# Decoding seven rows of a weight matrix straight into their buffer, and normalizing a first group of four tiles

## The chip, the cores and the metric

The kernel runs on 1 core of one Trainium2 chip. The metric is device time in microseconds (us); for the kernel before, the median of three runs is 979.46 us (975.63 to 984.27). Besides, one execution was taken by the hardware profiler.

## The reference, cut to what matters

Three layers follow one another on a batch of 4, 768 tokens, 8 heads of 40 (320 channels), all in float32:

```python
for t in range(S):                       # attention: a state per head, 768 steps
    y[:, :, t] = einsum('bhd,bhde->bhe', rt, state)
    Sa = einsum('bhde,bhe->bhd', state, at)
    state = state*wt[:, :, None, :] - einsum(Sa, bt) + einsum(vt, kt)
...
mixed = real(fft(fft(x, axis=1), axis=2))            # second layer
u = x + mixed
un = (u - mean(u)) / sqrt(var(u) + 1e-06)            # over the 320 channels
x = u + maximum(un @ w_ch1, 0) @ w_ch2               # 320 -> 1280 -> 320
...
u = x + (maximum(x.T @ w_tok1, 0) @ w_tok2).T        # third layer
out = u + maximum(u @ w_ch1, 0) @ w_ch2
```

The weights come as 64-bit floats. The kernel decodes each into two 32-bit parts, a rounded high part and the rest, and multiplies with both.

## The kernel before, in words

**Order.** The program is a list of operations (`Plan.op`: engine, cost, function, keys read and written). `Plan.emit` issues them in the sequence of a list written out by hand, `ORDER`: each entry is an operation's number in base 36, with the PSUM buffers that it takes; an entry `+5,acc,0` issues five filler pairs, matmuls of the identity that compute nothing (`warm`, line 54; each pair is two records in the trace). Every engine has its own queue and works it off in this order. An operation of engine `NONE` issues nothing; it opens or closes buffers, and other operations depend on it.

**Attention** (class `Attn`) runs in 12 chunks of 64 tokens, four chunks deep: `load`, `decay`, `kg`, `inv`, `merge`, `chain`, `outp`. Its buffers lie in pools that are closed at three points, the last of which is the operation 'end' in `Mlp.begin` (line 768 and on); the weights of the second layer, W1 and W2, have their buffers only from there on. While the attention runs, `wdec` decodes the first matrix (1280 columns) into DRAM.

**The second layer, per batch b.** `fft` (line 865) builds sums and differences on DVE, splits them into high and low parts (Xh, Xl) and multiplies with a table of cosines and sines on PE in five blocks (four main blocks, line 900, one tail, lines 915 and 916); ACT and DVE copy the result from PSUM into A (lines 925, 926). `fft2` (line 937) does the second transform in four PE groups ('mix', line 947, eight matmuls each) and adds it to x on DVE (line 950), with a sum per token; ACT squares (line 953) and accumulates the variance. Each of the six tiles of 128 tokens of the batch has its column in `sm` and `ss`. Then eight small steps on 6 columns (lines 960 to 967) give the factor `y` = 1/sqrt(var) with one correction step and the shift `nb`; the only ACT function of it is Sqrt (line 961). `norm` and `turnp` (lines 971, 1013) apply them and transpose a group of four tiles on PE (line 1018). `ch` (line 1026) multiplies the group with W1 (line 1047), takes the maximum with 0, splits, and multiplies with W2 (line 1037), ten blocks of 128 hidden channels each; block m reads row m of W2. There are six groups of four tiles; the FFT of the next batch runs inside the loop.

**The second matrix, W2, ten rows of 128 x 320.** `job` (line 844) decodes one row: a load on the SP queue into `mraw` (line 851), two DVE steps that build the value (853, 854), an ACT copy that rounds it to the high part `mdh` (855), two DVE steps for the low bits (856, 857), two POOL steps for the low part (858, 859), and two DMA writes on SP into DRAM (860, 861). There are three sets of buffers; row n uses set n mod 3. After 'end', POOL queues four DMA loads (line 795) that bring W2 back: five rows each of the high and the low part, each waiting for the ten writes of its rows. The third layer's matrices go through the same `job` afterwards.

Of the kernel before, what the change touches and what calls it, by code (L numbers as in the profile page):

```python
# [10 lines left out]
F32 = mybir.dt.float32  # L11
F32R = mybir.dt.float32r
# [84 lines left out]
class Attn:  # L97
    def __init__(s,tc,ident,A,xd,ctx,pctx,xstack,tstack,T1d,W):
# [74 lines left out]
    def decay(s,i):  # L173
# [362 lines left out]
0 1 5 4 2 fg 7 8 6 e 3 9 1b f g h +12,y,0 bx:0 1d 1f 1e a br 3s 1c 3u 8n 3v 3y 3w 7i 3t 7k 3x 3z j bk:1 by bz:0 bl i o m n k bm:1 bn b c d +3,y,0 s:0  # L536
c0 c1:1 l 1g 1h 1i 1l 8l 12:1 13 c2 p:0 1j 1k 40 1q x:2 q r t 1n y 1p bo:0 bp 1m 41 u:1 v w 1o z:0 10 14 15 11 7l +1,y,0 24:1 25 21:1 22 fa:1 fb bq 7m
16 1a 19 18 7n c3:0 c4 7q +1,y,0 1z:0 20 23 1u:2 1v 7r 7s 1w:0 1x 1y 1r:1 1s 26 27 28 1t 17 7o 8o 8p 8q 8v 8u 8t 29 2d 2e 2f 2g 2h 2i 2j 2k 2l 7j 2a
dq 2b 2c 8r fc:1 fd hi c8:1 ca fe:0 ff 7p 7v 7u 2m 2n 2o 2p 2q 2r 2t 2s 2u 2v 2x 2w 2y 2z 30 32 31 33 34 36 35 37 38 +13,y,0 c5:0 c7 kn 8m 8s 3a 39 7t
+10,y,0 7w:0 88:1 89 8b:1 8c 7z:1 8d 7x +1,y,0 85:0 dt ds 80 82:1 83 bs bt 3b 86 8e 8f 7y 8g 8j 8i 8k 8h hk dy du dr 3c dz 3e 84 81 8w 3d 8x 8y +7,y,0  # L540
8z:1 90 95:0 96 98:1 99 9b:0 9c 92:1 93 9e:0 9f 9j 3f 3i 3j 3g 3m 9i 3h 3n 8a bw 87 bv 3k dv dw c6 3l 3o e0 hl hr dx e3 e1 e2 9a hm 9h hq hn ho mp hs
ms 3r 3p 42 43 mt 9k 9o 9p 9q 9r 9s 9t 9u 9v 9w 9x 9y 9z a0 91 +12,y,0 e4:1 e5 +2,y,0 e7:0 e8 9n c9 3q a1 a4 a2 a3 a5 a6 a8 a9 aa a7 9l +2,y,0 ed:1 bu
b5 b3 b8:2 b9 ba bb bc bd fi b6 e9 ab ad b7 ee ef ac 44 9m b4 ew +2,y,0 ej:0 ek el +3,y,0 be:0 +1,y,0 bf bg bh ea:1 eg:0 et ey:1 ez ae af bi bj +2,y,0
cb:2 +2,y,0 ce:0 ex ah qj eb f0 +1,y,0 f1 94 e6 ag ai aj al hj hp eh en em ep 9d cc cd cf cg +2,y,0 ct:1 f3 cm:2 cn co ch:0 ck cl ci cj cp cq cr:0 f2
f4:1 f5 f6 +1,y,0 f7 cu ak am ap aq an at ao au eo es eq er cs cy:1 d6:0 cz cv:1 cw d0 hv d1 fy:0 hu ec fh eu ar as f8 d7 d8 ax ev ht g0 fv:2 of hw:0
i5:1 av 45 4a cx:0 ay aw b2 d9 fz 46 48 97 fx d2 i6 i7 i2:1 9g f9 hx d3:0 mq i3 i4 az b0 b1 ib:1 g4:0 d4 i8:0 gh:1 fw g1:1 47 49 4c 4d 4e 4g 4h 4b ic
id hz:1 g6 i9 g5 ia hy gi g3 k0 gj i0 i1 if ie g2 d5 gc:2 gf gg df:0 ig dg dh di gk 4f 4i 4j dc:1 dd fj fk fl fm gl:0 gm g7:0 ga gb da nw ih k5:1
# [757 lines left out]
```

## Time and profile before

| | us |
|---|---|
| median of three runs | 979.46 (975.63, 979.46, 984.27) |
| the profiled execution's own time | 969.72 |
| its span in the trace | 968.0 |
| PE busy | 914.7 |
| DVE busy | 702.4 |
| ACT busy | 491.8 |
| POOL busy | 367.6 |

Times in the trace are from the span's start. PE is TensorE, PEld its weight loads, DVE VectorE, ACT ScalarE, POOL GpSimd, SP the queue that issues most DMAs. Filler matmuls count as busy. The granted clock of PE is given as a share of 2.4 GHz; 0.50 is 1.2 GHz. The attention ends near 385 us, the second layer runs from there to 671 us, the third to the end.

### The profile page before, as it was taken

The page shows a single profiled execution, that of the slowest core. Times are in us where ns is not written, and L with a number is a line of the kernel's source. Part 1 is how long each engine was busy: PE and PEld are TensorE (multiplying, and loading weights), DVE is VectorE, ACT ScalarE, POOL GpSimd, SP SyncE. Part 2 cuts the span into 40 slices and gives each one's busy share as a digit, 9 for nine tenths or more (in the row PEclk, how much of TensorE's full clock was granted, in tenths as well). Part 3 has the DMA queues.
Part 4 walks back from the last instruction along what each step waited for, and adds up shares of the span by engine and source line. Part 5 has one row for each costly group of instructions (what it writes and reads, how often), then busy time and mean ns, then how long its engine had stood idle before and what let it go on. Part 6 is the DMA issues. An engine that isn't in the chain of part 4 may idle for free.

```text
span 968.0 us, 24200 instructions
## 1 busy us (share of the span) xinstructions
PE 914.7 (94%) x9657; PEld 848.1 (88%) x9657; DVE 702.4 (73%) x1527; ACT 491.8 (51%) x1068; POOL 367.6 (38%) x498
## 2 busy tenths in 40 slices
PE   6558999999999899899999999999999999999998
PEld 6557888888898789788888989989999999999998
DVE  6799598897959638898978665553686876766554
ACT  5265979797887655443434443323234343433422
POOL 5122526444364436334446552363233313132110
PEclk9788999999899989899999999999999999999999
DMA  9787898899777799846354423359442212303000
GB/s 213 155 169 174 174 196 215 180 199 203 170 183 171 180 242 286 287 140 194 126 172 123 151 86 109 132 166 374 144 175 86 80 50 79 101 1 99 1 28 28
DMA packets 153840, 146.15 MB, mean 151 GB/s; under 512 B 101695, under 2 KB 127359, under 8 KB 152959
## 3 DMA queue, kind: packets, MB, share of 16 engines
q1 hardware_dynamic: 143743, 117.64, 47.8%
q0 software_dynamic: 9984, 26.96, 9.1%
q8 instruction: 76, 1.25, 0.6%
q14 instruction: 37, 0.30, 0.1%
HBM read 96.22 MB, written 43.58 MB: 144 GB/s over the span
## 4 chain that ended last, share of the span: by engine, by line
PE 71%; DVE 9%; DMA 5%; ACT 3%; issue 2%; POOL 2%; SPq 1%; DVEq 0%; POOLq 0%; ACTq 0%
PE acc L1073 13%; PE hps L1047 9%; PE acc L1037 8%; PE sb L1084 7%; PE sa L1084 5%; PE sc L406 4%; PE kg L216 3%; PE warm L54 3%; PE tps L1179 2%; PE t2ps L1192 2%; PE y L428 1%; PE x L343 1%; PE s L367 1%; PE mix L947 1%; PE mg L291 1%
## 5 line engine op out<-in xcount | busy, mean ns | idle before, releaser
L1047 PE MATMUL hps<-cc,W1t 128*128 128x512 f32 x480 | 120.7, 395 | 0.0
L1037 PE MATMUL acc<-W,cc 128*128 128x320 f32 x720 | 116.1, 310 | 0.3 <-DMA W<-m11l 0.3
L1037 PEld LDWEIGHTS acc<-W,cc 128*128 128x128 f32 x720 | 109.0, 188 | 4.8 <-DMA W<-m11l 0.7
L1047 PEld LDWEIGHTS hps<-cc,W1t 128*128 128x128 f32 x480 | 87.9, 188 | 16.4
L1097 POOL TENSOR_TENSOR C<-C,C 128x256 f32<-128x256 f32 x36 | 27.4, 760 | 173.0 <-DVE W1t L1090 115.3
L1049 ACT ACTIVATE cc<-hps 128x512 fp32r<-128x512 f32 x60 | 35.8, 597 | 100.2 <-PE hps L1047 100.2
L1050 DVE SCALAR_TENSOR_TENSOR cc<-hps,cc 128x512 fp32r<-128x512 f32 x60 | 41.3, 688 | 56.6 <-ACT cc L1049 56.4
L54 PE MATMUL warm<-ident 128*128 128x128 f32 x454 | 74.2, 301 | 2.9 <-POOL ident masks.py:199 2.0
L216 PE MATMUL kg<-am,bt 120*128 120x192 f32 x242 | 55.7, 366 | 18.0 <-ACT am L136 15.7
L416 POOL TENSOR_SCALAR_AFFINE_SELECT sc<-sc 64x384 f32<-64x384 f32 (+1 forms) x72 | 42.3, 588 | 80.1 <-ACT sc L136 71.5
L225 POOL TENSOR_SCALAR_AFFINE_SELECT RT<-RT 64x384 f32<-64x384 f32 (+1 forms) x66 | 42.2, 659 | 78.4 <-ACT RT L136 77.2
L1091 DVE TENSOR_TENSOR C<-sb,C 128x256 f32<-128x256 f32 x108 | 44.2, 421 | 33.3 <-PE sb L1084 26.9
L54 PEld LDWEIGHTS warm<-ident 128*128 128x128 f32 x454 | 63.6, 207 | 5.2 <-POOL ident masks.py:199 2.0
L1073 PE MATMUL acc<-v,W1t 128*128 128x320 f32 x432 | 67.2, 309 | 0.0
L1073 PE MATMUL acc<-vb,W1t 128*128 128x320 f32 x432 | 66.9, 309 | 0.0
L1089 ACT ACTIVATE W1t<-C 128x256 fp32r<-128x256 f32 x108 | 41.9, 413 | 45.5 <-DVE C L1091 36.6
L1073 PEld LDWEIGHTS acc<-v,W1t 128*128 128x128 f32 x432 | 63.7, 188 | 0.1
L1073 PEld LDWEIGHTS acc<-vb,W1t 128*128 128x128 f32 x432 | 63.7, 188 | 0.0
L216 PEld LDWEIGHTS kg<-am,bt 120*128 120x128 f32 x242 | 43.0, 209 | 21.8 <-ACT am L136 16.8
L1090 DVE SCALAR_TENSOR_TENSOR W1t<-C,W1t 128x256 fp32r<-128x256 f32 x108 | 46.6, 450 | 19.4 <-ACT W1t L1089 19.0
L406 PE MATMUL sc<-rm,VZd 120*128 120x192 f32 x264 | 59.4, 358 | 0.3 <-ACT RT L136 0.3
L858 POOL TENSOR_TENSOR mda<-mda,mdh 128x320 f32<-128x320 f32 (+2 forms) x32 | 29.6, 933 | 72.2 <-ACT mdh L855 54.0
(223 smaller groups left out, 2253.1 us busy)
## 6 DMA issues: line engine op xcount, KB each, us to landing
bt<-in_bkR_dram SPq DMA_DIRECT2D x12, 660.0 KB
mdraw<-in_moe_w_ch_dram SPq DMA_DIRECT2D x22, 320.0 KB
mdraw<-in_moe_w_ch_dram SPq DMA_DIRECT2D x16, 384.0 KB
dr_T<-Y SPq DMA_DIRECT2D x24, 256.0 KB
Z<-dr_T SPq DMA_DIRECT2D x6, 1024.0 KB
wS<-in_wR_dram SPq DMA_DIRECT2D x12, 335.2 KB
a<-in_aR_dram SPq DMA_DIRECT2D x12, 335.2 KB
RT<-a SPq DMA_DIRECT2D x36, 111.7 KB
```

Of the source, the lines that this page charges most:

```text
L54: for x in range(m): nc.tensor.matmul(t[:,128*(x%4):128*(x%4)+128],lhsT=ident,rhs=ident,start=True,stop=True)
L216: nc.tensor.matmul(ps[:,192*x:192*x+192],lhsT=bt[:,g+x].rearrange("p v t -> p (v t)"),rhs=am[:,:,g+x],start=True,stop=True)
L225: nc.gpsimd.affine_select(out=kv,in_=kv,pattern=[[0,3*m],[1,L]],compare_op=ALU.is_gt,fill=0.0,base=0,channel_multiplier=-1)
L406: for x,g in enumerate(gs): nc.tensor.matmul(ps[:,192*x:192*x+192],lhsT=VZd[:,g].rearrange("p v t -> p (v t)"),rhs=s.rm[:,:,g],start=True, ...
L416: nc.gpsimd.affine_select(out=o,in_=o,pattern=[[0,3*m],[-1 if rv else 1,L]],compare_op=ALU.is_gt,fill=0.0,base=L-1 if rv else 0,channel_mu ...
L1037: nc.tensor.matmul(s.pst(acc[x]),lhsT=a[:,sl],rhs=w2(w,m),start=(m==0 and n==0),stop=(m==MT-1 and n==2))
L1047: for n,(l,r) in enumerate(ops): nc.tensor.matmul(ps,lhsT=l,rhs=r,start=n==0,stop=n==7)
L1073: nc.tensor.matmul(s.pst(acc[x]),lhsT=a[:,sl],rhs=wv(w),start=(u==0 and y==0 and k==0),stop=(u==5 and y==1 and k==2))
L1084: for n,(y,x) in enumerate(((0,0),(0,1),(1,0),(2,2))): nc.tensor.matmul(R[r](),lhsT=va(q,y),rhs=S[:,x],start=first and n==0,stop=last and ...
L1089: s.act(256,lambda: nc.scalar.activation(out=Hh(y,c),in_=src(),func=AF.Relu),rd,[('Hh',z,y,c)],free=free)
L1090: s.dve(.33,lambda: V.scalar_tensor_tensor(out=Hl(y,c),in0=src(),scalar=0.0,in1=Hh(y,c).bitcast(F32),op0=ALU.max,op1=ALU.subtract),rd+[('H ...
L1091: def add(n,r,m,free): s.dve(.33,lambda: V.tensor_tensor(out=C(n),in0=R[r](),in1=C(m),op=ALU.add),[K[r],('C',m)],[('C',n)],free=free)
```

## The change

Three edits, and the order list is written anew.

- Rows 3 to 9 of W2 are decoded into W2's buffer itself: the ACT copy writes the high part there and the last POOL step the low part; both wait for 'end' in addition. These rows are issued after 'end' in the program's numbering (not necessarily in the queues), and have no DMA writes. Rows 0 to 2 keep the way through DRAM; the four loads become two, of three rows each. `ch` waits for row m alone in place of a half.
- For batch 0 the small steps run twice: for the tiles 0, 3, 1, 4, whose sums are done first, and then for 2 and 5. The tiles of every batch are grouped in the sequence 0, 3, 1, 4, 2, 5. The correction takes one step less.
- At the program's start a memset and a Sqrt on one column are issued; the first masked copies of the attention (`am`) wait for it.

In the new order list PE's queue has, read by operation: 11 filler pairs before the last two main FFT blocks of batch 0 (before: 6), 7 before the first mix (5), 2 after the second mix (1), and 6, 9 and 4 between the fourth mix and the first matmul with W1 (9, 5, 6 and 1).

```diff
     def init(s):
+        s.one(s.sq1,['sq1']); s.P.op('ACT',.1,lambda: s.nc.scalar.activation(out=s.sq1,in_=s.sq1,func=AF.Sqrt),[],['sq1'])
...
-            s.act(.77,(s.am if i!=1 else s.rm)[:,h],a[:,:,:L],[ka,'hm'],[('am' if i!=1 else 'rm',h)],scale=s.hm[:,h:h+1])
+            s.act(.77,(s.am if i!=1 else s.rm)[:,h],a[:,:,:L],[ka,'hm']+['sq1']*(i==0),[('am' if i!=1 else 'rm',h)],scale=s.hm[:,h:h+1])
...
-        for k in range(10): s.job(k,"w2",[(slice(0,128),s.w[0][128*k:128*k+128])],h[:,k],l[:,k],TM+D2[0]+D2[1]*k)
+        for k in range(JD): s.job(k,"w2",[(slice(0,128),s.w[0][128*k:128*k+128])],h[:,k],l[:,k],TM+D2[0]+D2[1]*k)
...
         s.step(f,['mid'],['end'],after=attn)
+        s.P.stage=('dec2',0)
+        for k in range(JD,10): s.job(k,"w2",[(slice(0,128),s.w[0][128*k:128*k+128])],h[:,k],l[:,k],TM+D2[0]+D2[1]*k,direct=True)
...
-        for x in range(2):
-            for h in range(2): s.wload(lambda h=h,x=x: s.t["W2"][h][:,5*x:5*x+5],s.M1[1][h][:,5*x:5*x+5],['end']+[('mw',"w2",k,h) for k in range(5*x,5*x+5)],[('W2',h,x)],2.25)
+        for h in range(2): s.wload(lambda h=h: s.t["W2"][h][:,:JD],s.M1[1][h][:,:JD],['end']+[('mw',"w2",k,h) for k in range(JD)],[('W2',h,k) for k in range(JD)],.45*JD)
...
-        P.op('ACT',.09+d/1200,lambda: nc.scalar.activation(out=g("dh"),in_=g("da").bitcast(F32),func=AF.Copy),[ka],[kh],due=due)
+        oh=(lambda: s.t["W2"][0][:,n]) if direct else (lambda: g("dh")); ol=(lambda: s.t["W2"][1][:,n]) if direct else (lambda: g("da").bitcast(F32R))
+        en=['end'] if direct else []; kl=ka
+        if direct: kh,kl=('W2',0,n),('W2',1,n)
+        P.op('ACT',.09+d/1200,lambda: nc.scalar.activation(out=oh(),in_=g("da").bitcast(F32),func=AF.Copy),[ka]+en,[kh],due=due)
...
-        P.op('POOL',.07+d*.00237,lambda: nc.gpsimd.tensor_tensor(out=g("da").bitcast(F32R),in0=g("da").bitcast(F32),in1=g("dt").bitcast(F32),op=ALU.add),[kt],[ka],due=due)
+        P.op('POOL',.07+d*.00237,lambda: nc.gpsimd.tensor_tensor(out=ol(),in0=g("da").bitcast(F32),in1=g("dt").bitcast(F32),op=ALU.add),[kt]+([ka]+en if direct else []),[kl],due=due)
+        if direct: return
...
-        s.dve(.07,lambda: V.tensor_scalar(out=t["v"],in0=t["ss"],scalar1=320.0**-3,scalar2=1e-6,op0=ALU.mult,op1=ALU.add),[('ss',i) for i in range(6)],['lv'])
...
+        for c0,c1 in ((0,4),(4,6)) if b==0 else ((0,6),):
+            Y=lambda c0=c0,c1=c1: t["y"][b%2][:,c0:c1]; g=lambda n,c0=c0,c1=c1: t[n][:,c0:c1]; qs=TI[c0:c1]; z=c0//4
...
+            s.dve(.07,lambda g=g: V.tensor_scalar(out=g("v"),in0=g("ss"),scalar1=320.0**-3,scalar2=1e-6,op0=ALU.mult,op1=ALU.add),[('ss',i) for i in qs],kv)
+            s.act(54,lambda g=g,Y=Y: nc.scalar.activation(out=Y(),in_=g("v"),func=AF.Sqrt),kv,ky)
+            s.dve(.1,lambda Y=Y: V.reciprocal(out=Y(),in_=Y()),[],ky)
+            s.dve(.07,lambda g=g,Y=Y: V.tensor_tensor(out=g("q"),in0=Y(),in1=g("v"),op=ALU.mult),ky+kv,kq)
+            s.dve(.07,lambda g=g,Y=Y: V.scalar_tensor_tensor(out=g("q"),in0=g("q"),scalar=-0.5,in1=Y(),op0=ALU.mult,op1=ALU.mult),ky,kq)
+            s.dve(.07,lambda g=g,Y=Y: V.scalar_tensor_tensor(out=Y(),in0=g("q"),scalar=1.5,in1=Y(),op0=ALU.add,op1=ALU.mult),kq,ky)
...
-    def tiles(s,g): return [divmod(4*g+x,6) for x in range(4)]
+    def tiles(s,g): return [((4*g+x)//6,TI[(4*g+x)%6]) for x in range(4)]
...
-        k2=lambda m: [('W2',h,m//5) for h in range(2)]
+        k2=lambda m: [('W2',h,m) for h in range(2)]
...
+TI=(0,3,1,4,2,5)
...
+JD=3
```

## Rows read from the trace of the kernel before

**Rows 1.** The page's first part: busy us (share of the span) and instructions per engine.

```profile
PE 914.7 (94%) x9657; PEld 848.1 (88%) x9657; DVE 702.4 (73%) x1527; ACT 491.8 (51%) x1068; POOL 367.6 (38%) x498
```

**Rows 2.** Stretches: length, busy us (instructions) per engine, granted clock, DMA share, GB/s.

```profile
0.00:380.00 380.00, 338.13 (x5767) 302.83 (x5767) 296.84 (x560) 270.23 (x505) 159.53 (x251) 0.94 0.86 193
380.00:390.00 10.00, 9.21 (x103) 8.27 (x102) 9.71 (x23) 2.44 (x6) 3.13 (x8) 1.00 0.88 293
392.00:400.00 8.00, 5.08 (x26) 4.64 (x25) 6.95 (x16) 2.90 (x8) 2.02 (x2) 0.68 0.61 196
400.00:420.00 20.00, 19.77 (x147) 18.14 (x146) 16.66 (x52) 11.44 (x29) 7.48 (x10) 0.96 0.64 228
420.00:968.00 548.00, 540.54 (x3608) 512.43 (x3606) 370.25 (x878) 204.01 (x517) 193.83 (x227) 1.00 0.37 115
```

**Rows 3.** The same of line 54, the fillers, alone: PE, PEld.

```profile
0.00:380.00 380.00, 56.87 (x334) 47.83 (x334) 0.94 0.86 193
380.00:420.00 40.00, 14.54 (x104) 13.37 (x104) 0.91 0.72 245
```

**Rows 4.** The chain that ended last, 390 to 450 us: start, us, what.

```profile
394.51 2.82 PE psA L900 x13
398.18 2.50 PE warm L54 x10
400.68 2.90 PE mix L947 x16
...
449.06 1.19 PE mix L947 x8
```

**Rows 5.** Timeline, 394 to 420 us: start, us, what [idle before].

```profile
394.51 0.48 PE L900 MATMUL psA<-T,Xh 128*128 128x208 f32 x2 [2.06 <-DVE A L926]
397.75 0.38 DVE L926 TENSOR_TENSOR A<-psA,A 128x208 fp32r<-128x208 f32 x1 [0.84 <-ACT A L925]
405.90 0.19 ACT L953 ACTIVATION_READ_ACCUMULATOR sq<-X,sm 128x1 f32 x1
408.28 1.28 ACT L961 ACT_TABLE_LOAD   x1
408.76 2.19 PE L54 MATMUL warm<-ident 128*128 128x128 f32 x18
...
413.14 0.23 DVE L967 SCALAR_TENSOR_TENSOR nb<-sm,y 128x6 f32<-128x6 f32 x1
414.64 1.09 PE L1018 MATMUL trp<-ident,Y 128*128 128x128 f32 x8
419.20 3.98 PE L1047 MATMUL hps<-cc,W1t 128*128 128x512 f32 x16
```

**Rows 6.** The page's DMA issues: queue, count, KB each, us to landing.

```profile
m11h<-mdh SPq DMA_DIRECT2D x10, 160.0 KB
...
W<-m11h POOLq DMA_DIRECT2D x2, 800.0 KB, 6.5
```

**Rows 7.** PE's waits: who for whom, us in total, times, longest.

```profile
PE acc L1037 <- DMA W<-m11l: 0.3, 1, 0.3
```

**Rows 8.** Timeline, 366 to 389 us: decode steps, the attention's last read, the first load.

```profile
367.78 0.49 DVE L857 SCALAR_TENSOR_TENSOR mdt<-mdraw,mdt 128x320 f32<-128x320 uint16 x1
368.54 1.58 DVE L857 SCALAR_TENSOR_TENSOR mdt<-mdraw,mdt 128x320 f32<-128x320 uint16 x1
369.84 1.00 POOL L859 TENSOR_TENSOR mda<-mda,mdt 128x320 fp32r<-128x320 f32 x1
...
384.21 0.67 DVE L434 TENSOR_TENSOR X<-y,PT 64x240 f32<-64x240 f32 x2
385.41 1.05 POOL L795 DMA_DIRECT2D W1t<-m10h  x2 [3.90 <-DVE X L434]
388.40 0.90 DVE L854 SCALAR_TENSOR_TENSOR mda<-mdraw,mdt 128x320 int32<-128x320 int32 x2
```

**Rows 9.** ACT's first activation in the timeline.

```profile
8.14 0.23 ACT L136 ACTIVATE R<-Q 120x11 f32<-120x11 f32 x1 [6.05 <-DVE R L182]
```

More of the change, by code (lines that the diff above doesn't have):

```diff
@@ L660 @@
[L660 to L663 removed]
+5 6 0 1 7 4 fi 2 9 a 8 g 3 b 1d h i j +12,y,0 bz:0 1f 1h 1g c bt 3u 1e 3w 3x 8p 40 3y 7k 3v 3z 41 7m l bm:1 c0 c1:0 bn k p q o m bo:1 bp d e f n 1i 1j
@@ L664 @@
+3iu 3i4 3i8 3id 3ia 3ie 3i9 3hv 3hw 3hs 3ht 3in 3io 3iv 3ib 3ic 3ii 3ir 3if 3jd:10 3je 3jh 3is 3iw 3j1 3j2 3iy 3ji 3ig 3ih 3jb 3jf 3ij 3ik 3il 3im 3jc
+3ix 3jj 3j3 3j6 3jg 3jm 3jk 3jp 3jq 3j7 3iz 3j0 3j4 3j5 3jz 3j9 3ja 3jl 3jr 3jx 3jy 3j8 3k0 3ju 3jv 3jw 3js 3jt 3jn 3jo 3k2 3k3 3k1 3k4 3k7 3k8 3k9
+3ka 3k5 3k6 3kb 3kc
 """
@@ L780, in begin @@
         s.step(f,['mid'],['end'],after=attn)
+        s.P.stage=('dec2',0)
+        for k in range(JD,10): s.job(k,"w2",[(slice(0,128),s.w[0][128*k:128*k+128])],h[:,k],l[:,k],TM+D2[0]+D2[1]*k,direct=True)
+        s.P.stage=('mlp',0)
         def f():
@@ L949, in add @@
             def add(q,rows,cols):
-                s.dve(.46,lambda h=h: V.scalar_tensor_tensor(out=x(q,rows),in0=s.pst(h)[rows,cols],scalar=1.0,in1=x(q,rows),op0=ALU.mult,op1=ALU.add,accum_out=t["sm"][rows,q]),[kp]+xk(q)+['pend'],[('x',q,b),('sm',q)],free=[h[0]])
+                s.dve(.46,lambda h=h: V.scalar_tensor_tensor(out=x(q,rows),in0=s.pst(h)[rows,cols],scalar=1.0,in1=x(q,rows),op0=ALU.mult,op1=ALU.add,accum_out=t["sm"][rows,TI.index(q)]),[kp]+xk(q)+['pend'],[('x',q,b),('sm',q)],free=[h[0]])
             def mi(q,rows): add(q,rows,slice(320,0,-1))
             def stat(q):
-                s.act(710,lambda: nc.scalar.activation(out=t["sq"],in_=x(q),func=AF.Square,bias=t["sm"][:,q],scale=-320.0,accum_out=t["ss"][:,q]),[('x',q,b),('sm',q)],[('ss',q),'sq'])
+                s.act(710,lambda: nc.scalar.activation(out=t["sq"],in_=x(q),func=AF.Square,bias=t["sm"][:,TI.index(q)],scale=-320.0,accum_out=t["ss"][:,TI.index(q)]),[('x',q,b),('sm',q)],[('ss',q),'sq'])
             if i<3: add(i,slice(0,128),slice(0,320)); stat(i)
@@ L958, in fft2 @@
         s.first[b]=False
-        Y=lambda: t["y"][b%2]; NB_=lambda: t["nb"][b%2]
-        s.dve(.07,lambda: V.tensor_scalar(out=t["v"],in0=t["ss"],scalar1=320.0**-3,scalar2=1e-6,op0=ALU.mult,op1=ALU.add),[('ss',i) for i in range(6)],['lv'])
-        s.act(54,lambda: nc.scalar.activation(out=Y(),in_=t["v"],func=AF.Sqrt),['lv'],[('ly',b%2)])
-        s.dve(.1,lambda: V.reciprocal(out=Y(),in_=Y()),[],[('ly',b%2)])
-        s.dve(.07,lambda: V.tensor_tensor(out=t["q"],in0=Y(),in1=Y(),op=ALU.mult),[('ly',b%2)],['lq'])
@@ L964, in fft2 @@
-        s.dve(.07,lambda: V.tensor_tensor(out=t["q"],in0=t["q"],in1=t["v"],op=ALU.mult),['lv'],['lq'])
-        s.dve(.07,lambda: V.tensor_scalar(out=t["q"],in0=t["q"],scalar1=-0.5,scalar2=1.5,op0=ALU.mult,op1=ALU.add),[],['lq'])
-        s.dve(.07,lambda: V.tensor_tensor(out=Y(),in0=Y(),in1=t["q"],op=ALU.mult),['lq'],[('ly',b%2)])
-        s.dve(.07,lambda: V.scalar_tensor_tensor(out=NB_(),in0=t["sm"],scalar=-1.0/320,in1=Y(),op0=ALU.mult,op1=ALU.mult),[('sm',i) for i in range(6)]+[('ly',b%2)],[('nb',b%2)])
@@ L970, in tiles @@
-    def tiles(s,g): return [divmod(4*g+x,6) for x in range(4)]
+        for c0,c1 in ((0,4),(4,6)) if b==0 else ((0,6),):
+            Y=lambda c0=c0,c1=c1: t["y"][b%2][:,c0:c1]; g=lambda n,c0=c0,c1=c1: t[n][:,c0:c1]; qs=TI[c0:c1]; z=c0//4
+            kv=[('lv',y) for y in range(2)] if b else [('lv',z)]; kq=[('lq',y) for y in range(2)] if b else [('lq',z)]
+            ky=[('ly',b%2,y) for y in range(2)] if b else [('ly',0,z)]; kn=[('nb',b%2,y) for y in range(2)] if b else [('nb',0,z)]
+            s.dve(.07,lambda g=g: V.tensor_scalar(out=g("v"),in0=g("ss"),scalar1=320.0**-3,scalar2=1e-6,op0=ALU.mult,op1=ALU.add),[('ss',i) for i in qs],kv)
[4 more added lines that the diff above has]
+            s.dve(.07,lambda g=g,Y=Y: V.scalar_tensor_tensor(out=Y(),in0=g("q"),scalar=1.5,in1=Y(),op0=ALU.add,op1=ALU.mult),kq,ky)
+            s.dve(.07,lambda g=g,Y=Y,c0=c0,c1=c1: V.scalar_tensor_tensor(out=t["nb"][b%2][:,c0:c1],in0=g("sm"),scalar=-1.0/320,in1=Y(),op0=ALU.mult,op1=ALU.mult),[('sm',i) for i in qs]+ky,kn)
@@ L1153, in f @@
             p=s.m3s.enter_context(tc.tile_pool(name="m_v",bufs=1)); s.mk(p,[128,5,3,384],"vc",F32R)
-        s.step(f,[],[('W2',h,x) for h in range(2) for x in range(2)]+['m4'])
+        s.step(f,[],[('W2',h,k) for h in range(2) for k in range(10)]+['m4'])
         for q0,q1 in ((0,2),(2,5)): s.wload(lambda q0=q0,q1=q1: s.t["vc"][:,q0:q1],s.vS[:,q0:q1,:,384:],['m4'],[('vc',q) for q in range(q0,q1)],(q1-q0)*1152*512/360e3)
```

262 lines of the change are left out of this document (129 added, 133 removed).

## The prediction

> **What bounds the kernel now.** The profile's first part gives the engines: TensorE (PE) is busy for 94% of the span and VectorE (DVE) for 73% [rows 1]. Busy time alone misleads here, because PE's queue also holds filler matmuls (line 54) that compute nothing, so the second view splits the span into stretches [rows 2], and the third counts the fillers in them [rows 3]. From 420 us to the end PE works 540.54 of 548 us at the full clock with almost no filler: that stretch is bound by PE's own work, and whatever the change does there to DVE, ScalarE (ACT), GpSimd (POOL) or the DMA queues can win at most the 7.5 us in which PE idles. In the first 380 us PE is idle for 41.9 us and spends 56.87 us more on fillers: the attention loop is bound by chains through DVE and ACT. Between them, from 380 to 420 us, lies the hand-over, with 14.54 us of fillers. The first FFT, its normalization and the transposes before the first large matmul run there one after the other. All that this diff edits by hand lies in that stretch or feeds it, except the table instruction at the start.
>
> The fourth view, the chain of waits through the hand-over [rows 4], shows PE blocks of the FFT at 394.51, fillers at 398.18, the token mixes at 400.68. The fillers take 0.25 us a matmul there against 0.122 in the group at 408.76 [rows 5]: the granted clock is 0.68 in 392 to 400 us [rows 2], so part of it ran at 1.2 GHz. What PE did before: it sat idle 2.06 us until 394.51 [rows 5].
>
> **The change part by part**, against the profiled execution: span 968.0, time 969.72, which lies below all three timed runs (975.63 to 984.27, median 979.46). I carry the difference over to the median.
>
> **The trip through memory.** Seven of ten rows lose two writes of 160 KB each, and the reload falls from four transfers of 800 KB to two of 480 [rows 6]: 2,240 KB less each way, 14 issues less on SP, two less on POOL. Nothing on these queues ends last except the second reload: PE waits for it once, 0.3 us [rows 7]. That goes, because the last rows are decoded many microseconds before PE uses them. **-0.3 us.** The remaining traffic gets cheaper; no row shows a wait that this would shorten, so I take nothing for it.
>
> **The new wait.** Rows 3 to 5 may be written only after the attention's buffers are closed, whose last reader ends at 384.88; POOL passes that point at 385.41 [rows 8]. Behind the wait on ACT stand the copies that empty the FFT's PSUM, behind it on POOL the loads of the first matrix, and on DVE the first step of row 6, which reuses the buffers of row 3 and so needs row 3's last POOL step. POOL: 385.41, one load issue (half of 1.05), two steps of about 0.9 and 1.0: ready near 387.8. DVE came to its row steps at 388.40, so the wait is covered by 0.6 us; if the cover fails, each microsecond later is one of DVE's queue, and the FFT's copies stand in it. Two POOL steps of row 3 move from a time when DVE had gaps into 385 to 390, where DVE is busy 9.71 of 10 us [rows 2]. What such a meeting costs shows at 367.78 and 368.54: the same DVE step takes 0.49 alone and 1.58 where POOL's steps of 1.00 run beside it [rows 8], 1.09 more. So 0 to +2.2 for two steps. I take one meeting, **+1.1 us**, as some DVE steps in the stretch pass without one.
> The Trainium skill (SBUF — State Buffer, section "SBUF: two separate sides") says that DVE and GpSimd share one port pair, locked for a whole instruction, and that the loser blocks fully. The stretched step at 368.54 agrees; by that rule both steps would block, the term would be +2.2 and the sum 1.1 us worse.
>
> **Fillers ahead of the mixes.** The order list is rewritten throughout; read by operation it puts 11 filler pairs in place of 6 before the last two main FFT blocks, 7 in place of 5 before the first mix, 2 in place of 1 after the second. The five extra pairs, 10 matmuls of 0.122, fit into the 2.06 us of idle time [rows 5] and leave 0.84: no cost. What they do to the clock is the largest term. If PE keeps 2.4 GHz, the 13 block matmuls end earlier by as much as DVE can follow, and DVE idled 0.84 us for them at 397.75 [rows 5]; the fillers take 14 times 0.122, 1.7, in place of 2.50; the first two mixes two times 1.19, 2.4, in place of 2.90 [rows 4]. Together -0.84 - 0.8 - 0.5 = -2.1. If the clock falls as before, nothing is won and the two extra pairs cost 4 times 0.25, +1.0. I take **-2.1**: the nearest stretch with PE idle 0.8 us in ten, 380 to 390, shows a clock of 1.00 [rows 2]. The filler after the second mix: 2 times 0.122, **+0.25**.
>
> **First group and early table.** Today all six tiles' sums must be there: the fourth ends at 406.09, the table load begins at 408.28 and takes 1.28 us, the last factor starts at 413.14, the transposes at 414.64, the large matmul at 419.20 [rows 5]. With four tiles and the load already done the chain could start 408.28 - 406.09 = 2.2 us earlier and skip 1.28: 3.5 us. But PE cannot be early: between the fourth mix and 419.20 its queue holds fillers at four places, 42 matmuls, the group at 408.76 the largest [rows 5], and the new order still has 38 there (6, 9 and 4 pairs). PE is busy 19.77 of the 20 us from 400 to 420 [rows 2], so what the chain wins PE spends on fillers, and only 4 times 0.122 goes: **-0.5 us** (bounds 0 and -3.5). The early Sqrt and its memset cost nothing: ACT waits 6.05 us at the start before its first activation [rows 9]. The second, two-tile pass adds seven small steps on DVE and ACT, which those fillers cover; without the cover they would cost about a microsecond (seven at the 0.23 of the last factor is 1.6, and ACT holds one). One step less per later batch is hidden behind PE's full stretch.
>
> **The sum:** -0.3 + 1.1 - 2.1 + 0.25 - 0.5 = **-1.6 us**: 968.2 in the profiled execution, **977.9** at the median. The bounds together: -0.3 + 0 - 2.1 + 0.25 - 3.5 = -5.7 and 0 + 2.2 + 1.0 + 0.25 + 0 = +3.5. For the rest of the rewritten order, above all in the attention loop, no row gives a price. The slack it can eat or give back is the 41.9 idle and 56.87 filler us [rows 2, 3]; a tenth of those 99 us either way is 10 us, and since most runs of steps keep their order I take nothing.
>
> **The rivals.** A measurement here tells about 1%, 9.8 us, from no change.
> - *The chain is set free* (0.24). The fillers give way because PE was late anyway, the whole 3.5 is won, and the attention's rewritten order gives back a twentieth of its slack, 4.9: -0.3 - 2.1 - 3.5 - 4.9 = -10.8, so 968.7. For: DVE and ACT bound 99 us of the loop. Against: PE's queue order. It decides where the first transposes start: before 412 it is this one.
> - *The hand-over turns on DVE* (0.18). The POOL steps of rows 3 to 5 hold DVE between 385 and 392, the FFT's copies come later, PE's idle time before those two blocks stays near 2 us and the clock falls: +2.2 + 1.0 + 0.25 - 0.5 - 0.3 = +2.65, so 982.1, slower than before. For: DVE is full there. Against: the 0.6 us of cover. It decides when row 3's last POOL step ends after DVE has reached row 6.
> - *The loop loses* (0.12): the rewritten order opens gaps in the attention loop and costs a tenth of the slack, +9.9 and -1.6: 987.8.
> - *It does not do what it says* (0.03): ACT loads a table again before the first root and the group still waits for six tiles; then 979.5.
>
> **How the numbers follow.** The forecast keeps 0.43, with its own range 973 to 983. Faster by over 1%: most of the free chain (0.18) and a tail of the forecast (0.02). Slower by over 1%: most of the lost loop (0.10) and a tail of the DVE case (0.03). The range from 966 to 988 leaves out about one in ten on either side.
>
> **What would show each step.** In the changed kernel's profile: no table load after the start; no wait of the output matmuls of line 1037 for the reload; a clock near 1.00 in 392 to 400 us after its attention ends as here; fillers still touching each other between the fourth mix and the first large matmul, which then follows the fourth mix by some half a microsecond less than before; POOL's steps of row 3 right behind the buffers' closing. I am wrong if the time from the first large matmul to the end changes by more than 2 us, or if the attention part alone moves by more than 5.

## The result and the profile after

The changed kernel takes 978.86 us (median of 20 runs, 970.83 to 987.69) against 975.54 for the kernel before in the same rounds (20 runs, 962.58 to 987.62). The ratio is **1.0074, interval 1.0047 to 1.0100**: some 7 us slower. It leaves out, here and below, executions over 1.5% above a kernel's fastest (8 of the 20 before, 1 of the 20 after), which is why it lies above the ratio of the two medians, 1.0034 (3.3 us). The forecast was 977.9 with 1.6 us won; the time lies in the range, the sign is wrong.

The profiled execution: span 978.3, time 979.99. Its first part and, by stretches like those of [rows 2], length, busy us (instructions) of PE, PEld, DVE, ACT and POOL, clock, DMA share, GB/s. As the attention ends 7.8 us later here, the stretches begin 8 us later:

```profile
PE 922.8 (94%) x9687; PEld 856.5 (88%) x9687; DVE 718.2 (73%) x1529; ACT 492.4 (50%) x1069; POOL 366.9 (38%) x497
```

```profile
0.00:388.00 388.00, 344.11 (x5771) 308.00 (x5773) 298.51 (x561) 271.34 (x506) 153.68 (x250) 0.92 0.84 188
388.00:398.00 10.00, 8.95 (x99) 7.83 (x99) 9.69 (x18) 2.10 (x6) 5.02 (x8) 1.00 0.81 270
400.00:408.00 8.00, 4.89 (x37) 4.55 (x37) 7.75 (x15) 3.67 (x11) 4.08 (x6) 0.88 0.53 177
408.00:428.00 20.00, 19.69 (x142) 18.58 (x142) 18.91 (x55) 9.33 (x27) 7.54 (x9) 0.88 0.45 159
428.00:978.30 550.30, 543.80 (x3634) 516.14 (x3632) 381.40 (x879) 205.29 (x520) 196.56 (x226) 1.00 0.36 111
```

Two things differ from [rows 1, 2]. DVE has 15.8 us more work in all, with two instructions more (11.2 of it lies behind 428 us), and 18.91 of 20 us after the first mix where it had 16.66: its instructions got longer. And the attention lost more to the clock (0.92 against 0.94). The fillers of line 54 answer to [rows 3]:

```profile
0.00:388.00 388.00, 58.22 (x338) 49.99 (x338) 0.92 0.84 188
388.00:428.00 40.00, 15.88 (x114) 14.80 (x114) 0.91 0.58 197
```

Read from four marks (the last add of the attention, the first matmul with W1, the first matmul `tps` of the third layer, the 13th matmul `sa` behind it), the two profiles are:

| us | attention ends | hand-over to first W1 matmul | second layer | third layer's start | rest |
|---|---|---|---|---|---|
| before | 384.89 | 34.31 | 252.17 | 50.01 | 246.63 |
| after | 392.72 | 36.25 | 249.77 | 52.72 | 246.84 |

Behind the attention the change costs 1.94 - 2.40 + 2.71 + 0.21 = **+2.5 us**. These parts hardly vary: six profiles that have the code of before there show 34.2 to 34.3, 251.0 to 252.2 and 49.9 to 50.2, four with that of after (e1, e3 and e8 below) 36.2 to 37.8, 249.5 to 249.8 and 52.3 to 52.8. Between the means of the six and of the four the differences are +2.7, -1.8, +2.6 and -0.2, together +3.3. The hand-over, against [rows 4, 5]: the chain that ended last (start, us, what), then PE's timeline.

```profile
406.92 3.33 PE warm L54 x14
410.25 3.64 PE mix L954 x16
```

```profile
399.47 2.63 PE L54 MATMUL warm<-ident 128*128 128x128 f32 x22
403.71 0.47 PE L907 MATMUL psA<-T,Xh 128*128 128x208 f32 x2 [1.60 <-DVE A L933]
...
406.92 3.33 PE L54 MATMUL warm<-ident 128*128 128x128 f32 x14 [1.51 <-DVE A L933]
409.90 3.98 PE L954 MATMUL mix<-T,A 128*128 128x322 f32 x16
...
414.09 2.62 PE L954 MATMUL mix<-T,A 128*128 128x322 f32 x16
```

PE is idle 1.60 us before the third main FFT block (before: 2.06) and 1.51 before the fillers of the first mix (before: 0.86). From 406.1, in that second pause, the clock is down for 6.8 us: those 14 fillers and most of the first two mixes ran at 1.2 GHz. What held PE is in DVE's queue, beside POOL's:

```profile
392.05 0.67 DVE L435 TENSOR_TENSOR X<-y,PT 64x240 f32<-64x240 f32 x2 [0.16 <-PE y L429]
...
394.06 1.82 DVE L883 TENSOR_TENSOR FM<-X 128x960 f32<-128x960 f32 x1
395.81 1.15 DVE L857 SCALAR_TENSOR_TENSOR mda<-mdraw,mdt 128x320 int32<-128x320 int32 x1
...
401.24 0.88 DVE L895 TENSOR_TENSOR dd<-FM 32x161 f32<-32x161 f32 x1
402.15 1.10 DVE L889 TENSOR_TENSOR sd<-ef 128x353 f32<-128x353 f32 x1
...
405.21 1.15 DVE L883 TENSOR_TENSOR FM<-X 128x960 f32<-128x960 f32 x1
406.40 1.07 DVE L933 TENSOR_TENSOR A<-psA,A 64x208 fp32r<-64x208 f32 x3
407.49 1.00 DVE L897 TENSOR_TENSOR Ds<-dd,Ds 32x161 fp32r<-32x161 f32 x1
408.50 1.12 DVE L892 TENSOR_TENSOR Xl<-sd,Xh 128x353 fp32r<-128x353 f32 x1
409.55 1.19 DVE L892 TENSOR_TENSOR Xl<-ef,Xh 128x353 fp32r<-128x353 f32 x1
...
411.77 1.31 DVE L856 TENSOR_SCALAR mdt<-mdraw 128x320 int32<-128x320 int32 x1
```

```profile
393.83 1.03 POOL L864 TENSOR_TENSOR mda<-mda,W 128x320 f32<-128x320 f32 x1
394.95 1.66 POOL L865 TENSOR_TENSOR W<-mda,mdt 128x320 fp32r<-128x320 f32 x1
...
400.84 1.09 POOL L864 TENSOR_TENSOR mda<-mda,W 128x320 f32<-128x320 f32 x1 [3.71 <-ACT W L861]
402.01 0.85 POOL L865 TENSOR_TENSOR W<-mda,mdt 128x320 fp32r<-128x320 f32 x1
...
407.45 0.86 POOL L864 TENSOR_TENSOR mda<-mda,W 128x320 f32<-128x320 f32 x1 [3.01 <-ACT W L861]
408.38 0.86 POOL L865 TENSOR_TENSOR W<-mda,mdt 128x320 fp32r<-128x320 f32 x1
409.19 0.57 POOL L798 DMA_DIRECT2D W<-m11h  x1
...
410.30 1.16 POOL L864 TENSOR_TENSOR mda<-mda,W 128x320 f32<-128x320 f32 x1
...
412.01 0.88 POOL L865 TENSOR_TENSOR W<-mda,mdt 128x320 fp32r<-128x320 f32 x1
```

The first three rows of DVE and the first two of POOL answer to [rows 8]: behind the attention's last add (392.05) row 3's POOL steps run from 393.83 to 396.61, and the two DVE steps beside them take 1.82 and 1.15, where 1.15 (FM at 405.21) and 0.49 are usual. From 400.84 to 402.86 POOL works on row 4, and dd and sd beside it take 0.88 and 1.10. From 407.45 to 412.9 POOL is never free, with the steps of rows 6 and 5 and DMA issues between them, and the five DVE steps from 407.49 on (one of three Xl is left out above) take 1.00 to 1.31 each; shapes like these take 0.32 (Ds), 0.53 (Xl) and 0.32 (mdt) a few us earlier in the same queue. Between the attention's end and the first W1 matmul 9 DVE steps take over 1.5 times the shortest of their kind (before: 2), and all stretching together is 6.8 us (before: 2.1); what is left of DVE's work is equal, 32.3 in both, and POOL has 10 row steps there against 9. Their number hardly changed; what they stand beside did. That is more the order list's doing than the direct decode's: of the rows decoded directly only row 3's two steps came into this stretch, and rows 4, 5 and 6 had theirs there before too. But the new order has row 6's ACT copy behind all copies of the FFT, where it stood between them, so that POOL waits 3.01 us for it and row 6's steps begin 14.7 us behind the attention's end (before: 10.8), right ahead of row 5's.

PE's two pauses have different causes. The first, 1.60, shrinks to 0.48 in e5 below, where row 4's steps are gone from there. The second, 1.51, is in e5 as well, so it is not POOL's: the new order has DVE and ACT work off the first steps of the next batch (FM at 405.21, 1.15 us, and two copies Xh on ACT from 405.01) ahead of the FFT's last copies (`A` at 406.40). The five long steps behind them do not stop PE in this profile, whose mixes run slowly; they do in e8, at the end of this document.

The Trainium skill (SBUF — State Buffer, section "SBUF: two separate sides") has GpSimd and VectorE take a shared port pair for a whole instruction each. Four of the five agree: they end shortly behind a POOL step (408.49 behind 408.31, 409.62 behind 409.24, 411.85 behind 411.46, 413.08 behind 412.89). The fifth, at 409.55, began 0.3 us after POOL's step had ended, beside DMA issues (409.19, 409.75), and why it took 1.19 stays open: issues by themselves held no step (last section).

The table load is where it was meant to be, and the first root needs none:

```profile
0.80 1.28 ACT L143 ACT_TABLE_LOAD   x1 [0.80 <-PEq L1302]
...
417.66 0.20 ACT L971 ACTIVATE y<-v 128x4 f32<-128x4 f32 x1 [1.20 <-DVE v L970]
```

The rest against [rows 6, 7]: the transfers of the way through DRAM (queue, count, KB each, us to landing), and all of PE's waits in the second layer, 428 to 690 us (total, times, longest). Before, with that of the reload, its waits there made 2.7 us.

```profile
m11h<-mdh SPq DMA_DIRECT2D x3, 160.0 KB
...
W<-m11h POOLq DMA_DIRECT2D x1, 480.0 KB, 4.5
```

```profile
PE trp L1027 <- ACT Y L987: 0.7, 1, 0.7
PE trp L1027 <- DVE cc L1031: 0.2, 1, 0.2
```

### The profile page after: what moved, and what is told of

It reads as the page before. It is cut to its first block, busy times and chain, and to the rows that moved or that the text cites. A ratio compares the mean times of both kernels' runs of the same rounds, so it can differ in the third digit from the quotient of the medians.

```text
span 978.3 us, 24192 instructions
## 1 busy us (share of the span) xinstructions
PE 922.8 (94%) x9687; PEld 856.5 (88%) x9687; DVE 718.2 (73%) x1529; ACT 492.4 (50%) x1069; POOL 366.9 (38%) x497
## 4 chain that ended last, share of the span: by engine, by line
PE 73%; DVE 9%; DMA 5%; ACT 2%; issue 2%; SPq 1%; POOL 1%; DVEq 0%; ACTq 0%
PE acc L1082 13%; PE hps L1056 11%; PE acc L1046 10%; PE sb L1093 7%; PE sa L1093 5%; PE sc L407 4%; PE kg L217 3%; PE warm L54 2%; PE mix L954 2%; PE y L429 2%; PE x L344 2%; DVE pr L250 2%; DMA Mst<-Md 1%; PE tps L1188 1%; PE t2ps L1201 1%
## 5 line engine op out<-in xcount | busy, mean ns | idle before, releaser
L54 PE MATMUL warm<-ident 128*128 128x128 f32 x484 | 79.1, 303 | 3.6 <-POOL ident masks.py:199 2.1
L54 PEld LDWEIGHTS warm<-ident 128*128 128x128 f32 x484 | 69.3, 211 | 5.6 <-POOL ident masks.py:199 2.1
L226 POOL TENSOR_SCALAR_AFFINE_SELECT RT<-RT 64x384 f32<-64x384 f32 (+1 forms) x66 | 39.5, 617 | 86.4 <-ACT RT L136 83.7
L1100 DVE TENSOR_TENSOR C<-sb,C 128x256 f32<-128x256 f32 x108 | 44.5, 421 | 35.4 <-PE sb L1093 29.3
L407 PEld LDWEIGHTS sc<-rm,VZd 120*128 120x128 f32 x264 | 45.0, 203 | 6.2 <-issue 3.3
```

Source lines behind the costliest of these rows:

```text
L54: for x in range(m): nc.tensor.matmul(t[:,128*(x%4):128*(x%4)+128],lhsT=ident,rhs=ident,start=True,stop=True)
L407: for x,g in enumerate(gs): nc.tensor.matmul(ps[:,192*x:192*x+192],lhsT=VZd[:,g].rearrange("p v t -> p (v t)"),rhs=s.rm[:,:,g],start=True, ...
L1100: def add(n,r,m,free): s.dve(.33,lambda: V.tensor_tensor(out=C(n),in0=R[r](),in1=C(m),op=ALU.add),[K[r],('C',m)],[('C',n)],free=free)
```

## The experiments

16 runs followed, three of them (e8, e13, e14) repeats; a ratio is to the kernel before in the same rounds.

**Is it the loop or what follows it?** The one profile of after ends its attention 7.8 us later, at a place one can see: DVE applies the mask (`sc<-sc,tri`) at 104.87, 4 us later than before, PE waits 1.63 us for it, and from 105.7 the clock is at half for 10.2 us.

```profile
105.48 1.43 PE L217 MATMUL kg<-am,bt 120*128 120x192 f32 x4 [1.63 <-DVE sc L412]
```

So I exchanged the loop's part of the order list, and then only the mask's place (two DVE steps of an inverse ahead of it or behind it).

```diff
 e1_old_loop: after, with
-the order list's first part, to the transposes of the last attention chunk
+the same part from the list of before
 e2_new_loop: before, with that part from the list of after
 e3_mask_back: after, with
-... as ap aq av at au aw cu d0:1 ... cx:1 cy g0:1 ...
+... as ap aq av aw cu d0:1 ... cx:1 cy at au g0:1 ...
 e4_mask_late: before, with at au ahead of cy
```

> The changed kernel with the order of before for the attention loop (up to the last chunk's transposes) and its own order from there on. Theory A, the rewritten order of the loop lost the time: ratio to before 0.995 to 1.002, and in the trace no granted clock of 0.50 near 105 to 116 us, the attention's last read back near 385 us. Theory B, the hand-over and the later layers lost it: ratio stays at 1.005 to 1.010, the last read near 385 all the same, the rest 4 us or more longer than before.

> The kernel before with the changed kernel's order for the attention loop, its own code and order from there on. Theory A: ratio 1.005 to 1.010, the attention's last read near 392 us. Theory B: ratio 0.998 to 1.002.

> The changed kernel with two DVE steps of the inverse of chunk 1 (a product and its reduction) moved from ahead of the first mask of chunk 0 to behind it, as before. Theory A1, this one mask, which frees the PSUM buffer that the next kg matmuls need, starts the loss: PE's idle 1.63 us before kg near 105 us falls under 0.5, no clock of 0.50 near 106 to 116, the attention's last read 4 to 8 us earlier than in the changed kernel, ratio to before 0.999 to 1.004. Theory A2, many small shifts: the gap of 1.63 shrinks by no more than half a microsecond or comes back in the next kg, ratio 1.005 to 1.010.

> The kernel before with the same two DVE steps put ahead of the mask, nothing else. Theory A1: PE idles over 1 us before kg near 103 us, the clock falls there, ratio 1.004 to 1.009. Theory A2: the mask is 1 us later, PE idles under 0.6 us, the clock holds, ratio 0.999 to 1.002.

e1 1.0079 (1.0037 to 1.0122): with the old loop after is as slow as with the new, so the loop cannot be the whole of it. e2 1.0111 (1.0049 to 1.0172): yet the new loop by itself costs too. e3's profile ended its attention 6.5 us earlier than after's (386.18), as the mask theory has it, but its time stayed at 1.0108 (1.0054 to 1.0162); e4 lost nothing, 1.0022 (0.9989 to 1.0055). The mask theory, read from one gap of one profile, falls. The runs that test how much one profile says:

```diff
 e8_after_again: after, unchanged
 e13_before_itself: before, unchanged
 e14_loop_again: e2, unchanged
 e15_loop_mask: e2, with e3's edit
```

> The changed kernel unchanged, on the chip of the other three. If the loop's and the later parts' losses add up (each about 1.008 to 1.011 alone): ratio 1.012 to 1.02. If they don't add: 1.005 to 1.010. Profile: hand-over 36.2, second layer 249.7, third start 52.7 us again; the loop's end anywhere from 385 to 394.

> The kernel before against itself: how far a ratio of this job lies from 1 by chance, and a second profile of the old loop. Every theory: ratio 0.997 to 1.003, hand-over 34.3, second layer 251 to 252.2, third start 50.1. If the loop's spread alone makes the differences seen so far, its attention ends outside 381 to 390 us.

> The kernel before with the changed kernel's loop order, once more and in one job with the next run. Theory A (the loop's order loses): ratio 1.004 to 1.010, attention's last write 389 to 394 us. Theory B (only what follows the loop loses): ratio 0.998 to 1.002.

> The same with the two DVE steps behind the first mask again. If the mask is what the loop's order loses: ratio 0.997 to 1.003 and last write 381 to 388 us, 3 us or more faster than the run before this. If it only moves the gap: ratio 1.003 to 1.010.

e8 1.0059 (1.0022 to 1.0097), attention's end at 393.28 as in after; e13 0.9977 (0.9946 to 1.0008); e14 1.0016 (0.998 to 1.0053), against 1.0111 for the same kernel as e2 (the ratios of the medians, 1.0063 and 1.0066, are alike); e15 1.0047 (1.0014 to 1.0079), no faster than e14. The last add of the attention in e14, whose code is that of e2 (there it ended at 390.12); in e4 it ended at 380.81:

```profile
385.60 0.67 DVE L434 TENSOR_TENSOR X<-y,PT 64x240 f32<-64x240 f32 x2
```

Over the 18 profiles the attention ends between 380.8 and 396.6 (e13, the same kernel as before with its 384.89), and in all of them its end, less half of its time at 1.2 GHz, is 359 to 366: what differs most is how long the clock was down. **A single profile does not price the loop.** The executions together do better. Each has a mean clock and a span, so (1 - clock) times span is what it lost to the clock, and over 223 executions in 21 groups the time rises 0.69 us with each us of it (an estimate by least squares):

| loop order and rest | executions | mean us | lost to the clock | time less 0.69 of it |
|---|---|---|---|---|
| before, before | 96 | 970.5 | 26.4 | 952.1 |
| new, before (e2, e14) | 15 | 975.3 | 30.5 | 954.1 |
| new, new (after, e8) | 29 | 977.9 | 30.5 | 956.8 |

All kernels with the new loop order lost 30.3 (84 executions, standard error 0.5), all with the old one 26.3 (139, 0.3). By this the new loop costs 2.0 and, by the clock, 0.69 x 4.1 = 2.8; the parts behind it 2.7, as the profiles said (+2.5 and +3.3). Together 7.5, near the 7 of the ratio. e1 stands against this split: with the old loop it should be near 1.003, and its interval begins at 1.0037; e7, below, has it only at its edge. Which steps of the new loop order make the clock fall more is not shown.

**What holds DVE in the hand-over?** In e5 rows 4 to 6 leave ACT's and POOL's queues for places behind the first mixes. As the edit also moves their ACT copies, the loads and DVE's steps of row 7, it does not move POOL's steps alone.

```diff
 e5_rows_late: after, ACT and POOL queues
+first matrix's loads and W2's loads, then
 row 4's ACT copy behind the second tile's square, row 4's POOL steps
+rows 5 and 6 behind the fourth tile's square; row 7's DVE steps behind the
+second group's factors; row 9 behind the first W1 block's copies
```

> The changed kernel; the ACT and POOL steps of rows 4 to 6 (and what follows of rows 7 and 9) are queued behind the first mixes of the hand-over, and the last W1 and both W2 loads ahead of them. Theory C, DVE's steps meet POOL's steps and wait for them: from the attention's last write to the first large matmul 32 to 34.5 us in place of 36.25, the five DVE steps of 1.0 to 1.3 us ahead of the first mix back at 0.3 to 0.6, first mix 13.5 to 15.5 us after the last write in place of 17.18. Theory D, the fillers and the clock set the hand-over: the same steps shorten, but first mix stays later than 16.5 and the stretch at 35.5 or more.

The clock stays at 1.00 through the mixes, and the steps that took 1.00 to 1.19 take (Ds, the first of three Xl):

```profile
403.19 0.32 DVE L897 TENSOR_TENSOR Ds<-dd,Ds 32x161 fp32r<-32x161 f32 x1
403.52 0.53 DVE L892 TENSOR_TENSOR Xl<-sd,Xh 128x353 fp32r<-128x353 f32 x1
```

```profile
404.17 2.62 PE L954 MATMUL mix<-T,A 128*128 128x322 f32 x16
...
420.66 0.66 PE L1027 MATMUL trp<-ident,Y 128*128 128x128 f32 x4 [1.36 <-DVE cc L1031]
423.13 1.46 PE L954 MATMUL mix<-T,A 128*128 128x322 f32 x8 [0.92 <-DVE cc L1031]
```

The first mix starts 14.63 us after the attention (after: 17.18, before: 15.44) and the fourth ends at 20.06 (23.99, 21.27). So POOL's steps did hold DVE, and the rows in that place delayed PE. But of these 3.9 us 2.6 are given back before the first W1 matmul: the rows' work now stands on DVE where the transposes need its copies (waits of 1.36 and 0.92). The hand-over is 34.88, 0.4 above what was expected at most, and the second layer takes 250.85 in place of 249.77. Hand-over and second layer together are 285.7 (before 286.5, after 286.0). In time 976.74, one run, with 971.62 for before.

**What is direct decoding worth in this order?**

```diff
 e10_no_direct
-JD=3
+JD=10
-for h in range(2): load W2's rows :JD
+for x in range(2):
+    for h in range(2): load W2's rows 5x to 5x+5
```

> The changed kernel and its order, but all ten rows go through DRAM again (two writes a row, four loads of five rows), everything else as changed. If the direct decoding itself takes PE's waits out of the second layer: from the first large matmul to the third layer 250.8 us or more in place of 249.7, with a wait of the output matmuls for the reload; hand-over as before the edit (36 to 37.8), since the row steps on DVE, ACT and POOL stay where they are. If the rewritten order alone takes them out: 249.5 to 250.2.

989.92 (one run), hand-over 40.66, second layer 253.00. The second layer is as long as expected, but not for the wait that was expected: none of the output matmuls for the reload shows, PE waits for the copies `cc` of ACT and DVE (1.6 and 1.3 us). The hand-over is 3 us worse than expected, since a row's buffer must be written out before DVE may use it again, with the FFT's copies queued behind (`A`, for which PE then waits 5.3 us, 1.6 of them in after too):

```profile
423.56 0.49 DVE L858 SCALAR_TENSOR_TENSOR mda<-mdraw,mdt 128x320 int32<-128x320 int32 x1 [3.78 <-DMA m11l<-mda]
```

```profile
PE psA L908 <- DVE A L934: 5.3, 2, 3.7
```

Within this order the direct decode is worth 40.66 + 253.00 - 36.25 - 249.77 = 7.6 us, from one profile of each. The order of before, with the way through DRAM for all ten rows, reaches the same sum without it: 286.5 against 286.0.

**Why does the third layer start 2.7 us later?** The stretch from the first `tps` on holds 4 filler pairs before and 12 after (1.53 and 3.95 us of PE), and POOL's input comes late.

```diff
 e6_third_fill: after, with
-+3,acc,2 +1,acc,0 +1,acc,0 +2,acc,0 ... (12 filler pairs of the third layer's start)
 e9_third_old: after, with the third layer in the order of before and
-        for i in range(6):
+        for i in TI:     (the adds whose tiles the first group waits for)
```

> The changed kernel without the twelve filler pairs of the third layer's start (before has four pairs there). Theory F, these fillers stand on PE's path: from the first matmul of the third layer to the thirteenth of its last part 49.5 to 50.5 us in place of 52.72 (24 times 0.12 is 2.9). Theory W, PE waits there for DVE's adds and the fillers only fill the wait: 51.8 to 52.8, with PE idle in their place.

> The changed kernel with the third layer's queues in the order of before (no extra fillers), and with that layer's adds to x going through the tiles in the sequence 0, 3, 1, 4, 2, 5 in which the last part groups them. Theory G, the new grouping makes the last part's first group wait for the fifth tile that the third layer's product finishes: from its first matmul to the thirteenth of the last part 49.8 to 50.5 us in place of 52.72. Theory W2, another delay that the third layer inherits from the second: 51.8 or more.

Without the fillers 52.06 (one run, 978.89): PE idles in their place, they only fill a wait. In the order of before 51.97. After's load that POOL waits for, POOL's first step on it, and the same step before:

```profile
709.29 0.33 SPq L1000 DMA_DIRECT2D Z<-dr_T  x1
```

```profile
715.36 3.01 POOL L1005 TENSOR_TENSOR U<-Z 128x256 f32<-128x256 f32 x4 [7.67 <-DMA Z<-dr_T]
```

```profile
704.92 1.42 POOL L996 TENSOR_TENSOR U<-Z 128x256 f32<-128x256 f32 x2 [5.01 <-DMA Z<-dr_T]
```

After's load is issued 709.29 - 678.7 = 30.6 us behind the first `tps`, before's 700.09 - 671.4 = 28.7; POOL starts 6.07 us behind the issue, against 4.83. In e9 (one run, 977.89) the issue comes at 29.3, POOL's start 6.13 behind it. So theories F and G fall. The order accounts for 1.3 of the 1.9 us by which the issue is late, but for 0.75 of the 2.7 that the stretch is longer. The landing does not explain the rest in after's order: in e3, with the same third layer, POOL starts 5.27 behind the issue, and the stretch takes 52.73 all the same. In the order of before the two go together (e11, below: 4.98 and 50.79; e9, e12 and e16: 5.97 to 6.20 and 51.79 to 52.00). What costs the rest of the 2.7 stays open.

**A version that beats both?**

```diff
 e7_best: e1 + e5 + e6 (old loop, rows 4 to 6 late, no third-layer fillers)
 e11_best2: old loop, rows 4 to 6 late, rows 7 to 9 behind the first W1 blocks,
   third layer as e9
 e12_best3: e11 with the new loop and e3's edit
 e16_best4: after, with e3's edit, rows 4 to 6 late, rows 7 to 9 spread over the
   first two W1 blocks, third layer as e9
```

> The changed kernel with the loop order of before, the late rows and no third-layer fillers. If theories C and F both hold: hand-over 32 to 34.5, second layer 249.6, third start about 50, ratio to before 0.992 to 0.999, and 7 to 12 us below the changed kernel in the same job. If D and W hold: ratio 1.003 to 1.008.

> The changed kernel with the loop order of before, rows 4 to 6 behind the first mixes, rows 7 to 9 behind the first blocks of the large matmuls, and the third layer as in the run before this one. Hand-over 31.8 to 33 us (the mixes end near 20 after the attention's last write, and the 12.25 from there on no longer grow), second layer 249.5 to 250.5, third start about 50.1: 3 to 4.5 us less than before behind the loop, ratio 0.993 to 0.999. If a row step meets DVE's chain again elsewhere, hand-over 34 or more and ratio 1.000 to 1.004.

> As the run before this one, but with the loop order of the changed kernel in which only the two DVE steps stand behind the first mask again. If that mask is the loop's loss: the loop as with the order of before (the attention's last write at 381 to 388 us), ratio 0.993 to 1.000. If the loss is spread over the rewritten order: last write at 389 to 393, ratio 0.999 to 1.005.

> The changed kernel with the mask back, rows 4 to 6 behind the first mixes, the steps of rows 7 to 9 spread over the first two blocks of the large matmuls, and the third layer's order of before with its adds in the new grouping. Hand-over 32 to 33.5, second layer 249.5 to 251, third start 50.5 to 52: 2 us or so less than before behind the loop, ratio 0.995 to 1.001. If the spread steps hold up the copies of the large matmuls as in the two runs with all rows late: second layer over 253 and ratio 1.004 or more.

None does. e7 1.0050 (1.0019 to 1.0081), e11 1.0085 (1.0053 to 1.0117), e12 1.0113 (1.0069 to 1.0157), e16 1.0067 (1.0034 to 1.0101). e11 has the shortest hand-over of all, 32.54, and with e12 (261.22) the longest second layer, 260.18; e16 33.99 and 253.23. There the rows hold the copies out of PSUM (PE's waits in e11, 423 to 460 us):

```profile
PE acc L1046 <- DVE cc L1059: 3.5, 3, 1.8
PE acc L1046 <- ACT cc L1058: 3.1, 1, 3.1
```

Hand-over plus second layer: before 286.5, after 286.0, e5 285.7, e7 286.2, e16 287.2, e11 292.7, e12 295.2. In none of these places was the rows' work free; moving it moved the bill.

## Why the prediction was wrong

- **The step that failed: "Fillers ahead of the mixes", with its term of -2.1.** From the third main FFT block to the end of the fourth mix the time went from 11.65 to 13.0 us, +1.35 in place of a gain. It assumed that the FFT's copies keep pace on DVE and PE's idle time falls to 0.84; PE was idle 1.60 and 1.51 instead, and the clock fell all the same. In e5, with rows 4 to 6 moved away, that stretch took 10.2, 1.45 less than before, at 1.00: two thirds of the term. The step also carried a gain in the mixes to the end undiminished. e14, with the code of before from the attention on, ended its fourth mix 0.95 us sooner than before (20.32 behind the attention) and its hand-over 0.08 sooner; e5 passed on 1.4 of 3.9.
- **Part of its cause was on the list as the rival "the hand-over turns on DVE"**, with 982.1 for a chance of 0.18. The engine that it names is the right one; its place and its deciding point are not. It had POOL's rows 3 to 5 hold DVE between 385 and 392, up to 7 us behind the attention; there only row 3 did, with 1.3 us. Row 3's last POOL step ended at 396.61 and DVE came to row 6 at 398.86, so the wait was covered, by more than was forecast. The longer stretching came 8 to 10 us behind the attention, with row 4, and 15 to 20 us behind it, with rows 6 and 5. What the prediction had not followed is the new order there: it priced the two POOL steps of row 3, but not that row 6's would stand ahead of row 5's and both beside DVE's steps for the next batch, nor that these steps come ahead of the FFT's last copies. Each POOL step in that stretch, old or new, should have been laid beside the DVE step that runs with it.
- **The new wait, +1.1**: right in size, though it came as two meetings of 0.67 and 0.66 us and not as one of 1.1. The third main FFT block starts 10.99 us behind the attention's end in place of 9.62, +1.37; row 4's steps stretch DVE there by 1.1, as they did before, by 1.4.
- **First group and early table, -0.5**: right in size, -0.8 (12.25 us from the fourth mix to the first W1 matmul, before 13.04), and for the reason given: PE's queue spends the rest on fillers.
- **The trip through memory, -0.3**: too small. PE no longer waits for the reload, but its other waits in the second layer, for DVE's and ACT's copies, went as well (2.7 to 0.9 in all), and the layer takes 2.4 us less (1.8 in the mean of the profiles). The step "no row shows a wait that this would shorten" looked at waits for DMAs alone. Which of the removed pieces freed the copies is not shown one by one; e10, with the way through DRAM back, gives 3.2 us of the layer back.
- **"For the rest of the rewritten order ... I take nothing"**: wrong twice. The third layer's start costs 2.7 (0.75 by its own order, the rest open), in a stretch where the prediction saw only PE's full row of work; and the loop costs by the executions about 4 to 5, over half of it clock, with an interval from nothing (e14) to 1.7% (e2). The rival "the loop loses" had +9.9 for a tenth of the slack: right in sign, at half the price.
- **What would show each step**: no table load, no wait for the reload and fillers touching each other all came true. The clock near 1.00 did not (0.88; in e8, the same code, it was 1.00 there). Of the two signs of being wrong, the change from the first large matmul on stays under 2 us only because -2.4 and +2.7 cancel; the other, an attention part moved by more than 5, came with 7.8, but the ends of one kernel lie further apart than that (before and e13, 11.7).
- **Luck**: that 978.86 lies within 1 us of 977.9 is no merit of the sum. The forecast started from 979.46, the median of three runs, where twenty give 975.54; from there it would have been 974.0.

## What to carry to other kernels

A step moved off a slow path costs what it does to the engine beside it: look for every POOL step whose place moves, by the edit or by the order list, which DVE step on SBUF alone stands next to it, and who waits for that one. In a stretch that runs on two engines at once, look at hand-over and following stage as one sum, as gains in the first are often paid in the second. And a stage in which the clock falls has no price in one profile: here the same code ended its attention 4 us apart in two (e2, e14), half as far as before and after differ.

## What was not expected of the hardware

- POOL's steps hold DVE's steps on SBUF alone, but not those that read PSUM, and its DMA issues hold neither. Over the 18 profiles, from the attention's end to the third layer, 833 of 1190 SBUF-only DVE steps beside POOL's steps took over 1.4 times the shortest of their kind; of 1157 that read PSUM none did, and of 79 SBUF-only steps beside nothing but DMA issues none (steps and overlaps of 0.25 us or more). In e5 POOL issues seven DMAs from 393.37 to 397.21, and the DVE steps beside them keep their 0.32 to 0.66 us:

```profile
393.37 1.19 POOL L798 DMA_DIRECT2D W1t<-m10l  x2
```

```profile
394.83 0.53 DVE L892 TENSOR_TENSOR Xl<-sd,Xh 128x353 fp32r<-128x353 f32 x1
```

- One program has two hand-overs: after 36.25 and, the same code, e8 37.75. In the first the clock is down in the fillers and the first two mixes (3.33 and 3.98 us, above); in the second these run at 2.4 GHz, PE then waits 2.51 us for DVE's adds, which stand behind the five long steps, and the clock is down in the next two. The fourth mix ends 25.5 us behind the attention in place of 24.0, so a clock that holds did not by itself win the term of -2.1:

```profile
409.03 2.63 PE L954 MATMUL mix<-T,A 128*128 128x322 f32 x16
...
414.62 4.14 PE L954 MATMUL mix<-T,A 128*128 128x322 f32 x16 [2.51 <-DVE X L957]
```
